# Where the output-weight conversions of block 0 stand in ScalarE's queue: behind the Silu of two chunks earlier

## The chip, the cores and the metric

The kernel runs on one core of a Trainium2 chip. The metric is the device time of one launch in microseconds (us). Before the change it is 964.89 us, the median of three runs (964.42 to 965.96).

## What is computed

An attention layer and two gated feed-forward layers follow each other, all in float32. Attention has 4 batches, 8 heads, 576 positions and a head size of 64; four heads look at the last 32 positions, four at every 32nd. Its output, 2304 tokens of 512 numbers, goes through two layers with a hidden size of 1536:

```python
x  = attention(q, k, v)                                        # (2304, 512)
xn = x / sqrt(mean(x * x, -1) + 1e-6) * rms_g
x  = (silu(xn @ w_gate) * (xn @ w_val)) @ w_out                # layer 1
out = ((x @ w_a) * (x @ w_b)) @ w_out2                         # layer 2
```

## The kernel before

**Blocks and chunks.** Layer 1 runs over six blocks of 384 tokens (`t`, line 742) and, inside a block, over twelve chunks of 128 hidden units (`fc`, line 755). For a chunk, TensorE makes `g_ps` and `v_ps`, 12 matmuls each (lines 759 and 761), VectorE scales `g_ps` into `sg` (line 774), ScalarE applies Silu to `sg` (line 776), VectorE multiplies it into `v_ps` (line 787), and `split` makes two parts of the result, `hl`: ScalarE casts the high part (line 506), VectorE in block 0 and GpSimd later subtract it for the low part (line 507). `emit_y` then multiplies `hl` with the chunk's output weights, 12 matmuls into four accumulators `y`. It is called one chunk late (line 783). `g_ps` and `v_ps` share three PSUM buffers, so a `v_ps` can begin only when an earlier buffer was read.

**Three matmuls for one.** Every float32 operand is a high and a low part; `mm3` (lines 481 to 483) multiplies high by high, high by low and low by high.

**The conversions.** The weights arrive in a 64-bit layout and are made into such parts once, in block 0. `conversion` (line 153) has five instructions: on ScalarE an in-place Prelu (line 137) and a copy of a half word into the scratch tile `cz` (line 142), on VectorE a shift and or (line 145), on ScalarE the cast of the high part (line 150), on GpSimd the subtraction for the low part (line 151). The gate and value weights of a chunk are converted together by `convert1`, 1024 words a row, one chunk ahead (line 764). The output weights, 512 words a row, are converted at the end of a chunk's program text (lines 790 to 792), through a single scratch tile, and stored to DRAM for the later blocks (line 793). Their raw words of chunks 0 to 7 lie in pairs in `gv_raw`; those of chunks 8 to 11 go through two buffers `raw`, so that the load of chunk 10 waits for the shift of chunk 8, and that of chunk 11 for the shift of chunk 9.

**Attention in between.** While block `t` runs, attention for block `t + 1` runs between its chunks (`attention_slot`, line 781): scores, exponentials on ScalarE (lines 264 and 336), transposes through one PSUM buffer `att` (line 358), copies of these out to `pt` (line 368). Exponential, Silu and square root need different tables in ScalarE, and a table load stands wherever the kind changes.

**What sets the order.** Nothing is written in queue order. The framework's scheduler arranges the instructions of each engine with a model of their times; every engine then runs its queue strictly in that order. The text can only add edges: `tc.issue_after(i)` makes the instructions of a `with` block that run on the engine of `i` stand behind `i` in its queue. `gate` uses it for steps of attention, and `behind` for the Silus, whose instructions are collected in the list `silu`:

```python
with gate(fc + 1), behind(silu[:1] if fc > 1 else []):
    run(conversion(raw.pop((fc, 2)), wt, pool, engine(WLO[fc][2]), LOW[fc][2], True))
```

`silu[:1]` is the Silu of chunk 0. In block 0 the Silu of a chunk is appended before its conversion is traced.

**Afterwards** come blocks 1 to 5 with reloaded output weights, and layer 2 with a Strassen-like scheme of seven products.

Of the kernel before, what the change touches and what calls it, by code (L numbers as in the profile page):

```python
# [77 lines left out]
def fused_kernel(ctx: ExitStack, tc: tile.TileContext, qtl, ktl, vl, qs, ks, vs, cst, w1, w2, out):  # L78
# [7 lines left out]
    def engine(c):  # L86
        return {"P": nc.gpsimd, "D": nc.vector}[c]
# [65 lines left out]
    def conversion(third, ready, pool, lo_eng, low, out=False):  # L153

        st = {}
        n = ready.shape[1] // 2

        def z():
            if not st:
                st["z"] = pool.tile([128, (1 if out else 2) * DM], U32, tag=f"cz{out}", name="cz", bufs=NCZ[out])  # L160
            return st["z"][:, :n * DM]

        def last():
            x = z().bitcast(F32).rearrange("p (a n) -> p a n", a=n)
            hl = ready.rearrange("p (a s) n -> p a s n", s=2)
            parts(x, hl[:, :, 0], hl[:, :, 1], lo_eng)

        return words(third, z, low=low) + [last]

    def run(steps):  # L170
        for f in steps:
            f()
# [312 lines left out]
    def mm_in(ps, w, sel, x):  # L485
        for cc in range(NCC):
            c = slice(cc * 128, (cc + 1) * 128)
            mm3(ps, w[:, sel, 0, c], w[:, sel, 1, c], x[cc][:, 0], x[cc][:, 1], cc == 0, cc == NCC - 1)

    def tmp(name):  # L490
        return act.tile([128, NTB], F32, tag="t", name=name, bufs=NTMP)

    made = []
    silu, silu_gate = [], []

    @contextmanager
    def behind(instructions):

        with ExitStack() as e:
            for i in instructions:  # L500
                e.enter_context(tc.issue_after(i))
            yield

    def split(h, lo_eng):
        hl = act.tile([128, 2, NTB], F32R, tag="hl", name="hl", bufs=3)
        made.append(nc.scalar.copy(hl[:, 0], h).ins)  # L506
        made.append(lo_eng.tensor_tensor(hl[:, 1], h, hl[:, 0].bitcast(F32), op=ALU.subtract).ins)  # L507
        return hl
# [26 lines left out]
    def load_units(n):  # L535
        for which in units[:n]:
            raw.update(zip(which, load_pair(w1, which)))
        del units[:n]

    def load_late(which):  # L540
        raw.update(zip(which, load_pair(w1, which, pool)))

    def convert1(fc):
        t = gv[fc] = gv_slot(F32R, "gv")
        two = [raw.pop((fc, k)) for k in range(2)]
        if fc in FUSEDW:
            both, ready = gvraw[fc], t.rearrange("p k a n -> p (k a) n")
            run(conversion(both.rearrange("p k a n -> p (k a) n"), ready, pool, engine(WLO[fc][0]), LOW[fc][0]))
        else:
            run(zipped(*(conversion(two[k], t[:, k], pool, engine(WLO[fc][k]), LOW[fc][k]) for k in range(2))))  # L550

    def wo_tile():
        return wop.tile([128, 2, DM], F32R, tag="wo", name="wo", bufs=3)
# [27 lines left out]
    @contextmanager  # L581
    def gate(fc):

        with behind(silu[:1] if fc > 4 else []), ExitStack() as e:
            for key in GATES[min(fc, len(GATES) - 1)].split():
                e.enter_context(tc.issue_after(s0["st"][key].ins))
            yield
# [7 lines left out]
    def emit_y(t, fc):  # L595
        if fc == 0:
            for e in range(NCC):
                y[t, e] = psum.tile([128, 512], F32, tag=f"y{e}", name=f"y{e}")
        h = hl.pop((t, fc))
        w = wo.pop((t, fc))  # L600
        for e in range(NCC):
            c = slice(e * 128, (e + 1) * 128)
            mm3(y[t, e][:, :NTB], w[:, 0, c], w[:, 1, c], h[:, 0], h[:, 1], fc == 0, fc == NFC - 1)

    def evac_y(t):
        for e in range(NCC):
            if e % 2 == 0:
                both = act.tile([128, 2, NTB], F32, tag="x", name="ys", bufs=8)
            ys = both[:, e % 2]
            nc.vector.tensor_tensor(ys, y[t, e][:, :NTB], ri[t], op=ALU.mult)  # L610
            nc.sync.dma_start(x2d[t, e // 2][:, e % 2], ys)

    def load_wo(t, fc):
        wt = wo[t, fc] = wo_tile()
        nc.sync.dma_start(wt.rearrange("p a n -> p (a n)").bitcast(F32), wod[fc])
# [5 lines left out]
    def attention_slot(steps, fc):  # L621
        st = steps["strided"]
        n_sl = 10
        if t == 0:
            part = strided1.get(fc, "").split()
        else:
            part = st[len(st) * fc // n_sl:len(st) * (fc + 1) // n_sl] if fc < n_sl else []
        part += local[min(t, 1)].get(fc, "").split()
        part += ["rms", "rinv"] * (fc == n_sl)
        for n in part:  # L630
            steps[n]()

    def exps(steps):

        def together(f, key):
            def g():
                with behind([silu[-1]]):
                    f()
                silu_gate.append(steps["st"][key].ins)
            return g  # L640

        for n in ("lexp0", "lexp1", "lexp2"):
            steps[n] = together(steps[n], "exp")
# [98 lines left out]
    for t in range(NB):  # L742
        if t == 1:
            apool.close()
            pool = apool.enter_context(tc.tile_pool(name="attn", bufs=1))
        if t == NB - 1:
            apool.close()
            cpool.close()
            pool = p2.enter_context(tc.tile_pool(name="forms", bufs=1, reuse_waits="tile"))
            early = [f for k in (4, 5, 0, 1, 2, 3) for f in convert_forms(k, k < 4)]  # L750
        nxt = attention(t + 1, pool, psum, itertools.cycle(["att"])) if t + 1 < NB else None
        if t == 0:
            exps(nxt)
        x = [xt[t, cc] for cc in range(NCC)]
        for fc in range(NFC):
            if t > 0 and fc == 0:
                load_wo(t, 0)
            g_ps = psum.tile([128, 512], F32, tag="gv", name="g_ps", bufs=3)
            mm_in(g_ps[:, :NTB], gv[fc], 0, x)
            v_ps = psum.tile([128, 512], F32, tag="gv", name="v_ps", bufs=3)  # L760
            mm_in(v_ps[:, :NTB], gv[fc], 1, x)
            if t == 0 and fc + 1 < NFC:
                with gate(fc + 1):
                    convert1(fc + 1)
                if fc + 2 == NFC:
                    load_late([(NFC - 2, 2), (NFC - 1, 2)])
            if t == NB - 1:
                slab[fc] = wgt.tile([128, 4 * DM], F32 if fc in (0, 1, 11) else F32R, tag="gv", name="slab", bufs=NFC)
                with behind(made):
                    run(early[len(early) * fc // NFC:len(early) * (fc + 1) // NFC])  # L770
                    for k in [k for k in x0 if k <= fc]:
                        run(x0.pop(k))
            sg = tmp("sg")
            nc.vector.tensor_tensor(sg, g_ps[:, :NTB], ri[t], op=ALU.mult)  # L774
            with behind(silu_gate):
                silu.append(nc.scalar.activation(sg, sg, AF.Silu).ins)  # L776
            silu_gate[:] = []
            if fc == 1 and t > 0:
                evac_y(t - 1)
            if nxt is not None:  # L780
                attention_slot(nxt, fc)
            if prev is not None:
                emit_y(*prev)
            if t > 0 and fc + 1 < NFC:
                load_wo(t, fc + 1)
            h = tmp("h") if t else v_ps[:, :NTB]
            made[:] = [nc.vector.tensor_tensor(h, sg, v_ps[:, :NTB], op=ALU.mult).ins]
            hl[t, fc] = split(h, engine(HLO0[fc] if t == 0 else HLO[t]))
            if t == 0:
                wt = wo[0, fc] = wo_tile()  # L790
                with gate(fc + 1), behind(silu[:1] if fc > 1 else []):
                    run(conversion(raw.pop((fc, 2)), wt, pool, engine(WLO[fc][2]), LOW[fc][2], True))
                nc.sync.dma_start(wod[fc], wt.rearrange("p a n -> p (a n)").bitcast(F32))
                if fc % 2 and units:
                    load_units(1)
            prev = (t, fc)
# [240 lines left out]
```

## Time and profile before

| | value |
|---|---|
| median of three runs | 964.89 us |
| profiled execution, whole | 967.4 us |
| its span from first to last instruction | 965.6 us |
| TensorE busy (matmul) | 937.1 us, 97% of the span |
| VectorE, ScalarE, GpSimd busy | 621.5, 425.3, 539.5 us |
| mean granted TensorE clock | 0.985 |
| the chain that ended last | TensorE 65%, DMA 11%, VectorE 7%, GpSimd 7%, ScalarE 4% |

Block 0's chunks run from about 34 to 133 us of the span. The share of busy time is a mean over the whole kernel; a change in block 0 is read in block 0, from the waits of TensorE there.

### The profile page before, as it was taken

Reading aid. Unit: us, or ns where it says so; the run is one execution under the profiler, and the core shown is the slowest. Engines: PE = TensorE matmul, PEld = TensorE weight load, DVE = VectorE, ACT = ScalarE, POOL = GpSimd, SP = SyncE. Lnnn points to the kernel's source line nnn. Section 1 sums busy time; section 2 is a strip of 40 time slices with the busy share of each in tenths; the row PEclk is TensorE's granted clock in tenths of the full one; section 3 lists DMA queues with packets and bytes.
Section 4 is the critical chain, followed back from the end, with each engine's and each line's share of the span. In section 5 each row is a group of like instructions: output and inputs, shape, how many; then the busy total and the mean of one; then the engine's idle time right before and its main releaser. Section 6 shows DMA issues by size and latency. Waiting matters only on the chain.

```text
span 965.6 us, 14099 instructions
## 1 busy us (share of the span) xinstructions
PE 937.1 (97%) x5318; PEld 888.2 (92%) x5318; DVE 621.5 (64%) x900; ACT 425.3 (44%) x795; POOL 539.5 (56%) x407
## 2 busy tenths in 40 slices
PE   5998999999999999999999899999999999999998
PEld 4898999999999999999999898899999998999996
DVE  5658858658819895986666378658655655564534
ACT  5988646344433434434555455436425422122110
POOL 3567946558649677878479545655724423123211
PEclk6899999999999999999999999999999999999999
DMA  9974286537535563532788884996993974754701
GB/s 342 408 262 151 89 288 218 151 96 225 165 104 161 161 204 102 185 105 87 284 324 306 329 306 166 402 415 247 385 373 114 345 274 165 284 205 168 267 2 66
DMA packets 57363, 215.55 MB, mean 223 GB/s; under 512 B 5968, under 2 KB 14544, under 8 KB 51664
## 3 DMA queue, kind: packets, MB, share of 16 engines
q1 hardware_dynamic: 57296, 214.66, 61.3%
q8 instruction: 42, 0.69, 0.3%
q14 instruction: 25, 0.20, 0.1%
HBM read 172.17 MB, written 42.47 MB: 222 GB/s over the span
## 4 chain that ended last, share of the span: by engine, by line
PE 65%; DMA 11%; DVE 7%; POOL 7%; ACT 4%; issue 4%; SPq 0%; DVEq 0%; ACTq 0%; POOLq 0%
PE o L916 5%; PE o L918 5%; PE o L917 5%; DMA raw<-in_w 4%; POOL prod L248 4%; PE Y L862 4%; PE Y L861 4%; PE Y L860 4%; DMA gv_raw<-in_w 3%; PE y L482 3%; PE y L481 3%; PE g_ps L483 3%; PE y L483 3%; PE g_ps L482 3%; PE g_ps L481 3%
## 5 line engine op out<-in xcount | busy, mean ns | idle before, releaser
L151 POOL TENSOR_TENSOR hl<-c,hl 128x384 fp32r<-128x384 f32 x72 | 77.9, 1082 | 181.0 <-ACT hl L150 174.4
L248 POOL TENSOR_TENSOR prod<-kv_t,qs_t 128x512 f32<-128x512 f32 (+12 forms) x57 | 108.3, 1921 | 15.3 <-DMA kv_t<-in_ks 8.2
L481 PE MATMUL v_ps<-xx,gv 128*128 128x384 f32 x288 | 97.7, 339 | 1.9 <-DVE sg L774 1.8
L482 PE MATMUL y<-hl,wo 128*128 128x384 f32 x288 | 98.1, 341 | 1.1 <-POOL hl L507 1.1
L281 POOL TENSOR_TENSOR prod<-kv_t,S_t 128x512 f32<-128x512 f32 (+12 forms) x57 | 86.2, 1526 | 21.1 <-issue 7.1
L482 PE MATMUL v_ps<-xx,gv 128*128 128x384 f32 x288 | 97.9, 340 | 0.0
L483 PE MATMUL v_ps<-xx,gv 128*128 128x384 f32 x288 | 97.8, 340 | 0.0
L481 PE MATMUL g_ps<-xx,gv 128*128 128x384 f32 x288 | 97.5, 339 | 0.0
L483 PE MATMUL g_ps<-xx,gv 128*128 128x384 f32 x288 | 97.3, 338 | 0.0
L482 PE MATMUL g_ps<-xx,gv 128*128 128x384 f32 x288 | 96.9, 337 | 0.0
L867 DVE TENSOR_TENSOR c<-c,Y 128x384 f32<-128x384 f32 x108 | 59.0, 551 | 58.8 <-PE Y L862 53.5
L507 POOL TENSOR_TENSOR hl<-h,hl 128x384 fp32r<-128x384 f32 x60 | 64.1, 1069 | 58.4 <-ACT hl L506 57.3
L483 PE MATMUL y<-hl,wo 128*128 128x384 f32 x288 | 95.0, 338 | 0.0
L284 DVE TENSOR_REDUCE xs_t<-prod 128x64 f32<-128x448 f32 (+17 forms) x57 | 85.7, 1521 | 9.7 <-POOL prod L281 9.5
L481 PE MATMUL y<-hl,wo 128*128 128x384 f32 x288 | 85.0, 343 | 7.0 <-ACT hl L506 5.4
L916 PE MATMUL o<-slab,hl 128*128 128x512 f32 x216 | 84.7, 393 | 1.8 <-DVE slab L925 1.3
L917 PE MATMUL o<-slab,hl 128*128 128x512 f32 x216 | 84.5, 392 | 0.0
L918 PE MATMUL o<-slab,hl 128*128 128x512 f32 x216 | 83.2, 394 | 0.0
L150 ACT CAST hl<-c 128x384 fp32r<-128x384 f32 x72 | 37.0, 514 | 93.8 <-DVE c L897 93.5
L776 ACT ACTIVATE sg<-sg 128x384 f32<-128x384 f32 x72 | 38.0, 528 | 86.4 <-DVE sg L774 86.0
L862 PE MATMUL Y<-slab,form 128*128 128x384 f32 x216 | 73.0, 338 | 0.0
L861 PE MATMUL Y<-slab,form 128*128 128x384 f32 x216 | 73.0, 338 | 0.0
(137 smaller groups left out, 2491.4 us busy)
## 6 DMA issues: line engine op xcount, KB each, us to landing
form<-formd SPq DMA_DIRECT2D x32, 1792.0 KB, 10.7
wo<-wod SPq DMA_DIRECT2D x60, 512.0 KB, 3.8
raw<-in_w SPq DMA_DIRECT2D x40, 512.0 KB, 7.3
gv_raw<-in_w SPq DMA_DIRECT2D x32, 512.0 KB, 10.2
formd<-form SPq DMA_DIRECT2D x6, 1792.0 KB, 7.5
formd<-forms SPq DMA_DIRECT2D x6, 1792.0 KB, 12.8
slab<-x2d SPq DMA_DIRECT2D x24, 384.0 KB, 4.0
wod<-wo SPq DMA_DIRECT2D x12, 512.0 KB, 3.4
```

Source lines behind the costliest of these rows:

```text
L151: lo_eng.tensor_tensor(lo, x, hi.bitcast(F32), op=ALU.subtract)
L248: nc.gpsimd.tensor_tensor(pr, st["ks", g][:, :, :n, :], st["qs"][:, heads(g), mm:mm + 1, :].to_broadcast([128, G, n, D]), op=ALU.mult)
L281: st["pvm"] = nc.gpsimd.tensor_tensor(pr, st["vs", g][:, :, :n, :], st["S"][:, heads(g), mm, :n, None].to_broadcast([128, G, n, D]), op=AL ...
L284: st["pvr"] = nc.vector.tensor_reduce(st["xs"][:, mm, heads(g), :], pr.rearrange("p g n d -> p g d n"), axis=X, op=ALU.add)
L481: nc.tensor.matmul(out_ps, w_hi, x_hi, start=start, stop=False)
L482: nc.tensor.matmul(out_ps, w_hi, x_lo, start=False, stop=False)
L483: nc.tensor.matmul(out_ps, w_lo, x_hi, start=False, stop=stop)
L861: nc.tensor.matmul(bank(n), hi, x[p][:, 1, c], start=False, stop=False, skip_group_check=not begins)
L862: nc.tensor.matmul(bank(n), lo, x[p][:, 0, c], start=False, stop=c == 1, skip_group_check=not begins)
L916: nc.tensor.matmul(o, h[:, 0, cols], w[0], start=n == 0, stop=False)
L917: nc.tensor.matmul(o, h[:, 0, cols], w[1], start=False, stop=False)
L918: nc.tensor.matmul(o, h[:, 1, cols], w[0], start=False, stop=n == len(chunks) - 1)
```

## The change

From chunk 3 on, the ScalarE instructions of the output-weight conversion of chunk n must stand behind the Silu of chunk n - 2. For chunk 2 nothing changes: both rules name the Silu of chunk 0. Nothing is computed differently, and no instruction is added or taken away, except that the scheduler, given the new edges, arranges all queues anew up to the middle of block 1.

```diff
-                with gate(fc + 1), behind(silu[:1] if fc > 1 else []):
+                with gate(fc + 1), behind(silu[max(fc - 2, 0):max(fc - 1, 1)] if fc > 1 else []):
                     run(conversion(raw.pop((fc, 2)), wt, pool, engine(WLO[fc][2]), LOW[fc][2], True))
```

In the queues below, `sg_451`, `sg_529`, `sg_614`, `sg_847` and `sg_938` belong to chunks 0, 1, 2, 5 and 6; `hl_485` and `hl_891` to chunks 0 and 5; `v_ps_431` and `v_ps_509` to chunks 0 and 1. `gv_raw_179`, `gv_raw_188` and `gv_raw_197` hold the raw output weights of chunks 2 and 3, 4 and 5, 6 and 7, and `raw_203` those of chunk 8. The other `gv_raw`, 1024 wide, are gate and value weights.

ScalarE, from the Silu of chunk 0 to the cast of its result, before:

```order
L776 ACTIVATE sg_451<-sg_451 128x384
L137 ACTIVATE gv_raw_179<-gv_raw_179 128x512
L142 ACTIVATE cz_657<-gv_raw_179 128x512
L137 ACTIVATE gv_raw_179<-gv_raw_179 128x512
L137 ACTIVATE gv_raw_191<-gv_raw_191 128x1024
L137 ACTIVATE gv_raw_188<-gv_raw_188 128x512 x2
L776 ACTIVATE sg_529<-sg_529 128x384
L150 CAST gv_689<-cz_691 128x2x512
L137 ACTIVATE gv_raw_194<-gv_raw_194 128x1024
L506 CAST hl_485<-v_ps_431 128x384
```

and now:

```order
L776 ACTIVATE sg_451<-sg_451 128x384
L137 ACTIVATE gv_raw_179<-gv_raw_179 128x512
L142 ACTIVATE cz_657<-gv_raw_179 128x512
L137 ACTIVATE gv_raw_191<-gv_raw_191 128x1024
L776 ACTIVATE sg_529<-sg_529 128x384
L137 ACTIVATE gv_raw_179<-gv_raw_179 128x512
L150 CAST gv_689<-cz_691 128x2x512
L137 ACTIVATE gv_raw_194<-gv_raw_194 128x1024
L506 CAST hl_485<-v_ps_431 128x384
```

Two Prelus of 512 words (chunks 4 and 5) have left this stretch, and a third (chunk 3) moved behind the Silu of chunk 1.

VectorE at the same place, before:

```order
L787 TENSOR_TENSOR v_ps_431<-sg_451,v_ps_431 128x384
L145 SCALAR_TENSOR_TENSOR cz_657<-gv_raw_179,cz_657 128x512
L774 TENSOR_TENSOR sg_614<-g_ps_581,rinv_403 128x384
L787 TENSOR_TENSOR v_ps_509<-sg_529,v_ps_509 128x384
L507 TENSOR_TENSOR hl_485<-v_ps_431,hl_485 128x384
```

and now:

```order
L787 TENSOR_TENSOR v_ps_431<-sg_451,v_ps_431 128x384
L145 SCALAR_TENSOR_TENSOR cz_657<-gv_raw_179,cz_657 128x512
L787 TENSOR_TENSOR v_ps_509<-sg_529,v_ps_509 128x384
L774 TENSOR_TENSOR sg_614<-g_ps_581,rinv_403 128x384
L507 TENSOR_TENSOR hl_485<-v_ps_431,hl_485 128x384
```

The scaling of chunk 2 (line 774) now stands behind the product of chunk 1 (line 787), which waits for the Silu of chunk 1.

ScalarE, from the Silu of chunk 5 to the cast of its result, before:

```order
L776 ACTIVATE sg_847<-sg_847 128x384
L368 COPY pt0_114<-att_866 96x8x64
L142 ACTIVATE cz_1115<-gv_raw_725 128x1024
L137 ACTIVATE gv_raw_902<-gv_raw_902 128x1024
L776 ACTIVATE sg_938<-sg_938 128x384
L506 CAST hl_891<-v_ps_827 128x384
```

and now:

```order
L776 ACTIVATE sg_847<-sg_847 128x384
L137 ACTIVATE gv_raw_197<-gv_raw_197 128x512
L137 ACTIVATE gv_raw_902<-gv_raw_902 128x1024
L264 ACT_TABLE_LOAD
L264 ACTIVATE S_t_456<-S_t_456 128x72
L368 COPY pt0_114<-att_866 96x8x64
L142 ACTIVATE cz_1115<-gv_raw_725 128x1024
L776 ACT_TABLE_LOAD
L776 ACTIVATE sg_938<-sg_938 128x384
L137 ACTIVATE raw_203<-raw_203 128x512
L142 ACTIVATE cz_982<-gv_raw_197 128x512
L506 CAST hl_891<-v_ps_827 128x384
```

Two table loads, the exponential of the strided scores (line 264) and three instructions of the conversions of chunks 6, 7 and 8 now stand between the Silu of chunk 5 and the cast of its result; before, the exponential and its two table loads stood behind the casts of chunks 5 and 6. On TensorE the first four matmuls of chunk 5's `emit_y` stood ahead of `v_ps` of chunk 7 and stand behind it now.

## Rows read from the trace of the kernel before

**Rows 1.** Waits of TensorE, 33 to 140 us: us in total, times, longest.

```profile
PE y L481 <- ACT hl L506: 5.4, 3, 2.1
PE v_ps L481 <- DVE sg L774: 1.8, 3, 1.0
PE att L358 <- ACT pt L368: 0.7, 1, 0.7
```

**Rows 2.** Windows of TensorE: stretch, length, busy, granted clock, DMA share, GB/s.

```profile
53.00:57.00 4.00, 4.00 (x16) 0.57 1.05 401
90.50:94.50 4.00, 3.84 (x14) 0.57 0.73 262
131.00:135.00 4.00, 2.62 (x15) 1.00 0.73 235
```

**Rows 3.** Timeline of TensorE, 47 to 52 us: start, duration, instruction, idle before, releaser.

```profile
47.57 0.44 PE L481 MATMUL v_ps<-xx,gv 128*128 128x384 f32 x1 [0.65 <-DVE sg L774]
51.78 0.97 PE L481 MATMUL y<-hl,wo 128*128 128x384 f32 x4 [1.85 <-ACT hl L506]
```

**Rows 4.** Timeline of ScalarE, 45 to 52 us.

```profile
45.65 0.66 ACT L142 ACTIVATE cz<-gv_raw 128x512 uint32<-128x512 uint16 x1
46.20 2.80 ACT L137 ACTIVATE gv_raw<-gv_raw 128x512 f32<-128x512 f32 x4
48.87 0.55 ACT L776 ACTIVATE sg<-sg 128x384 f32<-128x384 f32 x1
...
51.23 0.50 ACT L506 CAST hl<-v_ps 128x384 fp32r<-128x384 f32 x1
```

**Rows 5.** Timeline of VectorE, 46 to 50 us.

```profile
46.96 0.56 DVE L774 TENSOR_TENSOR sg<-g_ps,rinv 128x384 f32<-128x384 f32 x1
49.45 0.56 DVE L787 TENSOR_TENSOR v_ps<-sg,v_ps 128x384 f32<-128x384 f32 x1 [1.93 <-ACT sg L776]
```

**Rows 6.** Waits of ScalarE, 33 to 140 us.

```profile
ACT s_t L336 <- DVE lmx L323: 2.7, 2, 1.7
```

**Rows 7.** Timeline of ScalarE, 84 to 95 us.

```profile
84.58 1.28 ACT L776 ACT_TABLE_LOAD   x1
85.87 0.53 ACT L776 ACTIVATE sg<-sg 128x384 f32<-128x384 f32 x1
...
87.82 1.12 ACT L137 ACTIVATE gv_raw<-gv_raw 128x1024 f32<-128x1024 f32 x1
88.83 0.51 ACT L776 ACTIVATE sg<-sg 128x384 f32<-128x384 f32 x1
89.25 0.45 ACT L506 CAST hl<-v_ps 128x384 fp32r<-128x384 f32 x1
...
93.86 0.27 ACT L264 ACTIVATE S_t<-S_t 128x72 f32<-128x72 f32 x1
```

**Rows 8.** Timeline of TensorE, 87 to 91 us.

```profile
87.01 0.61 PE L358 MATMUL att<-cst_sb,s_t 128*96 128x128 f32 x4 [0.71 <-ACT pt L368]
89.75 0.96 PE L481 MATMUL y<-hl,wo 128*128 128x384 f32 x4 [2.13 <-ACT hl L506]
90.88 0.69 PE L481 MATMUL v_ps<-xx,gv 128*128 128x384 f32 x1 [0.16 <-DVE sg L774]
```

**Rows 9.** Timeline of VectorE: end of the normalization, conversions of chunks 8 and 9.

```profile
96.33 0.23 DVE L273 TENSOR_TENSOR S_t<-S_t,srs 128x72 f32<-128x72 f32 x1
...
106.77 2.92 DVE L145 SCALAR_TENSOR_TENSOR cz<-raw,cz 128x512 uint32<-128x512 uint32 x1
...
118.68 1.32 DVE L145 SCALAR_TENSOR_TENSOR cz<-raw,cz 128x512 uint32<-128x512 uint32 x1
```

**Rows 10.** The end of block 0: timelines of ScalarE, the DMA queue and TensorE.

```profile
117.52 0.68 ACT L142 ACTIVATE cz<-raw 128x512 uint32<-128x512 uint16 x1 [1.70 <-POOL wo L151]
...
120.03 0.33 SPq L111 DMA_DIRECT2D raw<-in_w  x1
...
132.83 0.96 PE L481 MATMUL y<-hl,wo 128*128 128x384 f32 x4 [1.39 <-ACT hl L506]
```

## Prediction

> **What bounds the kernel now.** I read the page first: TensorE is busy 97% of the span, so only its idle time and its low-clock time can be won or lost. Then the waits of TensorE in block 0 [rows 1]: 5.4 us for the casts of `hl`, 1.8 us for the scaling that frees a PSUM buffer, 0.7 us for a copy of the transposes. The windows [rows 2] show what else is lost: in 53 to 57 us and in 90.5 to 94.5 us the granted clock was 0.57, a stretch at the lower level, 1.2 GHz, in each; everywhere else in the chunks it was at or near 2.4 GHz. One such stretch costs 43% of 4 us, about 1.7 us of work. Before the first TensorE had stood still 1.85 us in one piece [rows 3], before the second 2.13 us and 0.71 us [rows 8]; the idle 1.39 us at the end of the block [rows 10] was followed by a clock of 1.00 [rows 2]. So all that block 0 can give is some 8 us of waits and 3 us of clock. From 135 to 240 us the list of TensorE's waits is empty, and the queues differ only up to the middle of block 1 (some 190 us), so a lead or lag at 133 us should go through to the end.
>
> The sum is made against the profiled execution, 967.4 us with a span of 965.6; the median of the runs, 964.89, is 2.5 below it, and I carry the difference over. About 0.2%, 1.9 us, is what a measurement of this kernel can tell from no change.
>
> **The first place, chunks 0 to 2.** ScalarE's stretch from the Silu of chunk 0 to the cast of its result loses two Prelus of 512 words. One such piece takes 0.55 us from start to start (45.65 to 46.20) [rows 4]. So the cast moves from 51.23 to 50.1 us, 1.1 us earlier, and the Silu of chunk 1 (three Prelus fewer ahead of it) from 48.87 to 47.2. That alone would take 1.1 us from the wait of 1.85 us. But VectorE now does the product of chunk 1 first, and that waits for this Silu: 47.2 and 0.55 for the Silu [rows 4] is 47.75, the product 0.5 to the next start, then the scaling of chunk 2, 0.56 [rows 5], ends at 48.8 where it ended at 47.5 before. `v_ps` of chunk 2 waits for exactly this scaling and so starts 1.3 us later than 47.57 [rows 3]. TensorE's idle time is therefore 0.65 + 1.30 = 1.95 us in one piece ahead of `v_ps`, and none ahead of `y`, whose `hl` has been ready since 50.6: 1.95 against 0.65 + 1.85 = 2.50 us. **Gain 0.55 us**, bounds 0 (the Silu no earlier) and 1.1 (the product does not hold the scaling). A still stand of 1.95 us lies between the two that came before a fall (1.85, 2.13) and above the one that did not (1.39), so I let the clock fall as before, at no gain.
>
> **The second place, chunks 5 to 7.** Ahead of the Silu of chunk 5, ScalarE has three Prelus fewer in its queue than before (chunks 7, 8 and 9), 1.7 us; its waits for the scores, 2.7 us in all [rows 6], take part of that back, since those come from TensorE and VectorE. Between 0 and 1.7 I take 0.9: the Silu at 85.0 instead of 85.87 [rows 7]. Behind it the queue got longer. The cast of chunk 5's `hl` came 3.38 us after the Silu (85.87 to 89.25). Now two table loads of 1.28, an exponential of 0.27 and three conversion pieces of 0.55 come on top: 3.38 + 2.56 + 0.27 + 1.65 = 7.9 us, so 92.9 us.
>
> More of this lies on TensorE's path. The copy to `pt`, which frees the buffer of the transposes, comes after the exponential: 85.0 + 0.42 (Silu) + 0.55 + 1.01 (the wide Prelu, 87.82 to 88.83) + 1.28 + 0.2 = 88.5, done at 89.0 us. TensorE would be done with chunk 7's `g_ps` at 86.30 - 0.55 = 85.75 and waits 3.4 us instead of 0.71 [rows 8]. After 0.61 us of transposes `v_ps` of chunk 7 waits for its scaling, which stands on VectorE behind the normalization of the strided scores. That ran from 94.13 (end of the exponential) to 96.56 [rows 7, 9] with a product of 0.5 in it; without that some 1.8 us: 88.7 + 1.8 + 0.56 is 91.0, against 90.88 before. So the lead is gone there, and the first four matmuls of chunk 5's `y`, 0.96 us, which ran inside the wait before, come after. **Lag behind before: about 1 us**, that is 1.5 us lost here. Bounds: nothing lost if the Silu leads by 1.7 us, 2.4 lost if by none. The clock falls here before and after: once each, at no cost.
>
> The Trainium skill has a rule against just this: its page ScalarE: Activation LUTs, section "Table sets: the hidden batching unit", says to do all functions of one set before switching, and section "What ACT_TABLE_LOAD costs" gives 1283 ns for the load and about 1380 ns for a drain. The trace agrees with the load (1.28 us) and not with the drain: the Silu starts 0.01 us after the load ends [rows 7]. By the Trainium skill's 2.66 us for each switch the pair would put another 2.8 us, an estimate, on the path.
>
> **The end of the block.** Before, TensorE stood 1.39 us for the cast of chunk 11 [rows 10]. That wait takes up a lag of up to 1.39 us as long as the cast does not come later. Its chain begins with the shift of chunk 9 (118.68, [rows 9]), which frees the buffer for the load of chunk 11 (120.03), and runs over the conversions of chunks 10 and 11, the square root and two table loads, one after the other, to 132.83. The shift itself waited for chunk 8's subtraction on GpSimd, 1.70 us [rows 10]. In the new queue of GpSimd two score products stand ahead of the conversions instead of between them, so this wait can shrink; but all else arrives 1 us later. I take the cast as 0.4 us earlier; bounds 1.7 earlier (no wait), 1.6 later (the shift takes 2.92 instead of 1.32 us, as chunk 8's did [rows 9]). TensorE is free at 131.4 + 1.0 = 132.4, and the cast is there at 132.4. **Sum: +0.55 - 1.5 + 1.39 of cover, so 0.4 us gained**, 964.89 - 0.4 = 964.5 us. The other edits (queues of block 1, two reloads of output weights issued later) I cost at nothing: TensorE has no wait there, and it would show as a new one.
>
> **Rivals.** *The clock holds at the first place.* The still stand comes in one piece ahead of `v_ps`, with full work around it. If it does not bring the lower clock, 1.7 us are won on top of 0.55. ScalarE's chain lets not all of it through; with 1.8 us of 2.25 the time is 963.1. Against it: both falls of before followed a pause of about this size. Chance 0.27.
>
> *ScalarE becomes the bound between the Silus of chunks 5 and 6* and the kernel is slower. If the Silu of chunk 5 does not lead, `v_ps` of chunk 7 starts at 91.9, the lag is 1.9 us, and TensorE has stood still some 5 us in two pieces instead of 3.0, so that a second low-clock stretch of 1.7 us follows. 3.6 us less 1.39 of cover is 2.2 more: 967.1 us. It decides from the point where the lag passes 1.39 us, a Silu of chunk 5 later than about 85.4. For it: the scores set ScalarE's pace [rows 6]. Chance 0.15.
>
> *The shift of chunk 9 is held up by GpSimd*, as chunk 8's was (2.92 us). The cast then comes 1.2 us late instead of 0.4 early: 966.1 us. Against it: chunk 9's took 1.32 before. Chance 0.10. The Trainium skill (page SBUF — State Buffer, section "SBUF: two separate sides") has VectorE operations with two SBUF inputs and GpSimd share one port pair that the first holds for its whole instruction; the trace has both durations, and does not show the port.
>
> *A table switch costs more than its row*, a pause as long as the load after each: 2 x 1.28 more, at 1.0 + 2.56 - 1.39 a lag of 2.2: 967.1. Nothing in the trace speaks for it; chance 0.02. The drain that the Trainium skill states (ScalarE: Activation LUTs, "What ACT_TABLE_LOAD costs") would be such a pause.
>
> **How the numbers follow.** The forecast, 964.5, has 0.46, with its own range from 963.5 to 965.8. The first rival straddles the bound of 1.9 us: 0.18 of its 0.27 I count as faster, and 0.08 of the forecast through its bounds. So faster 0.26; slower takes the second rival, the fourth and a part of the others, 0.21; same 0.53. Leaving out 2 in 10 the range is 962.4 to 967.2.
>
> **What would show it.** Right: the wait ahead of `v_ps` of chunk 2 about 1.95 us and none ahead of the first `y`; the cast of chunk 5 about 7.9 us after its Silu; a wait of some 3.4 us for the copy to `pt`; the last wait of block 0 short or gone; the end of the block within 1 us of 132.8. Wrong: a clock near 1.00 in 50 to 57 us, or a third low stretch, or new waits in block 1 for reloaded weights.

## The result, and the profile after

The changed kernel takes 974.34 us (median of four runs, 972.54 to 975.19), the kernel before on the same chip 965.42 us (964.42 to 966.67). The ratio is 1.0086, 95% interval 1.0071 to 1.0101: **slower by about 8.3 us** (8.9 by the medians), where 964.5 was forecast and 967.2 was the upper end of the range. The profiled execution took 972.54 us with a span of 970.8, mean granted clock 0.987.

The waits of TensorE from 33 to 200 us, in the profile of the changed kernel (us in total, times, longest):

```profile
PE att L358 <- ACT pt L368: 3.8, 1, 3.8
PE v_ps L481 <- DVE sg L774: 3.2, 3, 1.7
PE att L296 <- DVE s_t L314: 1.5, 1, 1.5
PE y L481 <- ACT wo L150: 1.5, 1, 1.5
PE g_ps L481 <- DVE sg L774: 1.3, 1, 1.3
PE att L358 <- DVE s_t L348: 1.0, 1, 1.0
PE y L482 <- POOL hl L507: 1.0, 2, 0.5
PE y L481 <- DVE ys L610: 0.4, 1, 0.4
PE att L412 <- ACT sq L432: 0.2, 1, 0.2
```

Against [rows 1]: the 5.4 us for the casts of `hl` are gone, 3.8 us for the copy to `pt` have come, and seven kinds of wait are new. Four of these, 3.9 us, lie in block 1, where the list of before was empty; none of them is for reloaded output weights (`wo` at 113 us is chunk 8's conversion in block 0). The first two windows of [rows 2]:

```profile
53.00:57.00 4.00, 4.00 (x25) 1.00 1.05 403
90.50:94.50 4.00, 4.00 (x19) 0.70 0.54 179
```

The clock held at the first place and fell at the second. The timeline of TensorE at its longer waits:

```profile
48.13 0.45 PE L481 MATMUL v_ps<-xx,gv 128*128 128x384 f32 x1 [1.73 <-DVE sg L774]
...
82.39 0.41 PE L481 MATMUL g_ps<-xx,gv 128*128 128x384 f32 x1 [1.28 <-DVE sg L774]
...
88.53 0.61 PE L358 MATMUL att<-cst_sb,s_t 128*96 128x128 f32 x4 [3.79 <-ACT pt L368]
...
89.44 0.67 PE L481 MATMUL v_ps<-xx,gv 128*128 128x384 f32 x1 [0.29 <-DVE sg L774]
...
113.45 0.44 PE L481 MATMUL y<-hl,wo 128*128 128x384 f32 x1 [1.46 <-ACT wo L150]
...
156.18 1.15 PE L296 MATMUL att<-k_t,q_t 128*64 128x64 f32 x16 [1.49 <-DVE s_t L314]
...
172.33 0.61 PE L358 MATMUL att<-cst_sb,s_t 128*96 128x128 f32 x4 [1.01 <-DVE s_t L348]
```

ScalarE at the second place, to set beside [rows 7]:

```profile
84.26 0.53 ACT L776 ACTIVATE sg<-sg 128x384 f32<-128x384 f32 x1
...
86.36 1.28 ACT L264 ACT_TABLE_LOAD   x1
...
87.83 0.56 ACT L368 COPY pt<-att 96x512 f32<-96x512 f32 x1
...
89.45 1.28 ACT L776 ACT_TABLE_LOAD   x1
90.74 0.53 ACT L776 ACTIVATE sg<-sg 128x384 f32<-128x384 f32 x1
...
92.33 0.45 ACT L506 CAST hl<-v_ps 128x384 fp32r<-128x384 f32 x1
```

**Where the lag arises.** Two milestones place it. The first is the start of `v_ps` of block 1's second chunk, with all of block 0 behind it: 137.12 us before and 137.60 now, a lag of 0.5. The second is a scaling in the middle of block 1, after which the two queues agree to the end; the timeline of VectorE has it before, and then in the changed kernel, as

```profile
200.59 0.56 DVE L774 TENSOR_TENSOR sg<-g_ps,rinv 128x384 f32<-128x384 f32 x1 [1.78 <-PE g_ps L483]
```

```profile
206.27 0.56 DVE L774 TENSOR_TENSOR sg<-g_ps,rinv 128x384 f32<-128x384 f32 x1 [1.78 <-PE g_ps L483]
```

a lag of 5.7. So of the pair of profiled executions block 1 costs 5.2 us, and block 0 next to nothing. That pair flatters block 0: the execution of before had lost some 1.6 us to the clock at the first place, which the changed one had not.

The listed waits of block 1 sum to 3.9 us; most of the rest of the 5.2 lies at the same stops, which cost more than the list counts. The 12 matmuls of one `y` took 2.08 us up to the next `g_ps` before (175.02 to 177.10 us) and take 2.88 now (179.90 to 182.78), with a listed wait of 0.51.

How block 1 loses this shows on VectorE. In the changed kernel's timeline, the fourth evacuation of block 0's output stands behind a reduction of strided scores, and two normalizations behind reductions of strided products:

```profile
135.36 1.48 DVE L610 TENSOR_TENSOR ys<-y,rinv 128x384 f32<-128x384 f32 x3
140.01 0.62 DVE L251 TENSOR_REDUCE S_t<-prod 128x7 f32<-128x448 f32 x1 [3.17 <-POOL prod L248]
140.55 0.55 DVE L610 TENSOR_TENSOR ys<-y,rinv 128x384 f32<-128x384 f32 x1
...
170.64 1.00 DVE L284 TENSOR_REDUCE xs_t<-prod 128x64 f32<-128x512 f32 x1
171.56 2.03 DVE L348 TENSOR_TENSOR s_t<-s_t,lrs 128x384 f32<-128x384 f32 x2
```

Before, all four evacuations ran ahead of that reduction, and the normalizations ahead of the first reduction of strided products, which began at 165.81 us:

```profile
136.41 1.94 DVE L610 TENSOR_TENSOR ys<-y,rinv 128x384 f32<-128x384 f32 x4
...
163.67 1.15 DVE L348 TENSOR_TENSOR s_t<-s_t,lrs 128x384 f32<-128x384 f32 x1
```

GpSimd's first product of the block waits for a load of keys. The queue of DMA issues (SP) now has a reload of output weights between two of the three key loads; the first row is of before, the others of the changed kernel:

```profile
132.86 1.70 SPq L236 DMA_DIRECT2D kv_t<-in_ks  x3
...
133.39 1.19 SPq L236 DMA_DIRECT2D kv_t<-in_ks  x2
134.68 0.37 SPq L615 DMA_DIRECT2D wo<-wod  x1
135.09 0.43 SPq L236 DMA_DIRECT2D kv_t<-in_ks  x1
```

The product starts at 138.82 us (137.75 before), 1.1 later. The first key load was issued 0.5 later anyway, so about half of this goes with the reload; no run tried it alone.

### The profile page after: what moved, and what is told of

It is laid out like the page before. It is cut to its first block, busy times and chain, and to the rows that moved or that the text cites. A ratio compares the mean times of both kernels' runs of the same rounds, so it can differ in the third digit from the quotient of the medians.

```text
span 970.8 us, 14102 instructions
## 1 busy us (share of the span) xinstructions
PE 936.3 (96%) x5318; PEld 886.0 (91%) x5318; DVE 622.7 (64%) x900; ACT 424.4 (44%) x795; POOL 542.6 (56%) x407
## 4 chain that ended last, share of the span: by engine, by line
PE 65%; DMA 9%; POOL 8%; DVE 8%; ACT 4%; issue 4%; SPq 0%; POOLq 0%; DVEq 0%; ACTq 0%
PE o L916 5%; PE o L918 5%; PE o L917 5%; POOL prod L248 4%; DMA raw<-in_w 4%; PE Y L862 4%; PE Y L861 4%; PE Y L860 4%; PE y L482 3%; DMA gv_raw<-in_w 3%; PE y L481 3%; PE y L483 3%; PE g_ps L483 3%; PE v_ps L481 3%; PE v_ps L483 3%
## 5 line engine op out<-in xcount | busy, mean ns | idle before, releaser
L248 POOL TENSOR_TENSOR prod<-kv_t,qs_t 128x512 f32<-128x512 f32 (+12 forms) x57 | 106.3, 1888 | 25.6 <-DMA kv_t<-in_ks 18.2
```

The source lines that it names most:

```text
L248: nc.gpsimd.tensor_tensor(pr, st["ks", g][:, :, :n, :], st["qs"][:, heads(g), mm:mm + 1, :].to_broadcast([128, G, n, D]), op=ALU.mult)
```

## The experiments

All kernels but e6, e9 and e10 differ from the kernel before only in the Silu behind which the conversion of a chunk queues; a table in the line of the change says it, and a chunk that the table does not name stays behind the Silu of chunk 0:

```diff
-  behind(silu[:1] if fc > 1 else [])
+  behind(silu[{3: 1, 4: 1, 5: 1}.get(fc, 0):][:1] if fc > 1 else [])
```

Theory A puts more than half of the loss into block 1's new order; theory B puts it into block 0, between the Silus of chunks 5 and 6. Which order block 1 takes follows from the scheduler, and some tables leave it as before while others change it; that made the parts separable.

| run | table or edit | median us | ratio to before, 95% interval | lag at the two milestones, us |
|---|---|---|---|---|
| the change | n - 2 | 974.34 | 1.0086 (1.0071 to 1.0101) | 0.5, 5.7 |
| e1 | 3, 4, 5: 1 | 965.79 | 0.9997 (0.9989 to 1.0006) | -2.3, -2.3 |
| e2 | as e1, 7: 5 | 967.11 | 1.0015 (1.0006 to 1.0023) | -0.1, -0.1 |
| e3 | 8: 6, 9: 7 | 971.41 | 1.0055 (1.0043 to 1.0067) | 2.6, 5.5 |
| e4 | 7: 5 | 966.98 | 1.0012 (1.0003 to 1.0020) | -0.7, -0.7 |
| e5 | 3: 1, 4: 2, 5: 3, 8: 6, 9: 7 | 968.90 | 1.0030 (1.0020 to 1.0040) | 1.8, 1.9 |
| e6 | the change, one edge more in block 1 | 973.75 | 1.0074 (1.0057 to 1.0091) | 3.0, 8.0 |
| e7 | 3: 1, 4: 2, 5: 2 | 968.74 | 1.0029 (1.0019 to 1.0040) | 2.0, 2.0 |
| e8 | 3, 4, 5: 1, 6: 3 | 967.53 | 1.0012 (1.0001 to 1.0024) | 0.2, 0.2 |
| e9 | the change, block 1: local steps first | 971.68 | 1.0062 (1.0045 to 1.0079) | 1.3, 3.7 |
| e10 | before, block 1: local steps first | 965.91 | 1.0002 (0.9986 to 1.0018) | -2.3, -2.3 |
| e11 | 3, 4, 5: 1, 11: 11 | 963.35 | 0.9974 (0.9960 to 0.9988) | order differs, -3.9 |
| e12 | 11: 11 | 963.13 | 0.9982 (0.9968 to 0.9996) | order differs, -3.3 |

A lag is of one profiled execution against that of before. Executions of the same queue differ by up to 1 us at the start of block 0, and by some 1.6 us more where the clock held at the first place, so the difference of a row's two lags says more than either.

**e1, the first place alone.**

> Chunks 3, 4 and 5 behind the Silu of chunk 1, all later ones behind that of chunk 0 as before: the queues differ from before on ScalarE and VectorE between the Silu of chunk 0 and that of chunk 2, and nowhere else. Theory A (the loss of the change was made in block 1's new queues) and theory B (it was made between the Silus of chunks 5 and 6) both expect the gain of the first place alone: if the clock holds there as in the profile of the changed kernel, 2.5 us less than before (962.9); if it falls in most runs, as in the prediction, 0.5 less (964.9). Theory C (the first place itself is worth nothing or costs over many runs): 965.4 or more.

No gain over the runs. The wait ahead of `v_ps` of chunk 2 was 1.72 us, as in the change, but 0.55 us for `hl` of chunk 0 stayed, since another order of ScalarE's pieces than in the change stands ahead of that cast. The profiled execution held its clock; e10, with the queue of before, held it as well. That is theory C's number, and the gain of 2.5 us is ruled out; a gain of 0.5 us lies inside the interval. The place is worth nothing that can be measured.

**e2 and e4, the exponential moved ahead with and without the first place.** The table of e4:

```diff
-  behind(silu[:1] if fc > 1 else [])
+  behind(silu[{7: 5}.get(fc, 0):][:1] if fc > 1 else [])
```

> As e1, and chunk 7 behind the Silu of chunk 5: the exponential of the strided scores now stands between the Silus of chunks 5 and 6, as in the change, and block 1 keeps the order of before. Theory A: the loss of the middle of block 0 is small, within 1 us of e1. Theory B: the loss between the Silus costs the 3.8 us that the profile of the change shows from 56 to 134 us: 3 to 4 us more than e1.

> Chunk 7 behind the Silu of chunk 5, the others as before: the first place and block 1 are those of before, the exponential stands between the Silus of chunks 5 and 6. Theory A: within 1 us of before (964.5 to 966.5). Theory B: 3 to 4 us slower (968.5 to 969.5).

Both lose 1.2 to 1.4 us, and nothing in block 1. Theory A's size is right within half a microsecond; B's 3 to 4 us do not come. In these two the copy to `pt` stands ahead of the exponential, and TensorE waits only 1.26 and 1.23 us for it. It also waits 1.54 us for a scaling ahead of a `g_ps` and 2.01 for the one ahead of `v_ps` of chunk 7: 4.8 us at this place in both, against 3.0 in the kernel before [rows 8] and 5.4 in the change.

**e3, the late chunks alone.** Table `{8: 6, 9: 7}`.

> Chunks 8 and 9 behind the Silus of chunks 6 and 7, the others as before: the first place is that of before, the exponential stands between the Silus of chunks 5 and 6, and block 1 has the new order of the change. Theory A: 4 to 5 us slower than before by block 1's waits alone, 969.5 to 970.5 and up. Theory B: as slow, but with the lag already there at the end of block 0. The lag at 134 us tells them apart: under 1.5 us for A, 3 or more for B.

The time is as both expected, and neither has the place: 2.6 us at the end of block 0 and 2.9 more in block 1. Both theories have a half of it. Its order of block 1 is not quite that of the change, as the expectation had it: VectorE's two normalizations stand behind three reductions of strided products instead of five, and the wait of 1.01 us at 172 us is absent.

**e5, block 1 given back its order.** Chunks 6, 7, 10 and 11 return to the Silu of chunk 0:

```diff
-  behind(silu[max(fc - 2, 0):max(fc - 1, 1)] if fc > 1 else [])
+  behind(silu[{3: 1, 4: 2, 5: 3, 8: 6, 9: 7}.get(fc, 0):][:1] if fc > 1 else [])
```

> The change for chunks 3, 4, 5, 8 and 9; chunks 6, 7, 10 and 11 stay behind the Silu of chunk 0. The first place is that of the change, the exponential stands between the Silus of chunks 5 and 6 and ahead of the copy to pt as in the change, but block 1 has the order of before. Theory A (more than half of the loss is block 1's new order): within 2 us of e2, 966 to 969. Theory B (the loss is made in block 0 behind the Silu of chunk 5): close to the change, 972 to 975.

2.9 us slower than before instead of 8.3: more than half of the loss went with block 1's order. (Block 0 is not exactly that of the change either: the wait of 1.46 us for chunk 8 is absent, and the one ahead of `v_ps` of chunk 7 is longer.) All waits of its TensorE from 33 to 200 us:

```profile
PE v_ps L481 <- DVE sg L774: 4.8, 3, 1.9
PE att L358 <- ACT pt L368: 3.9, 1, 3.9
PE y L481 <- ACT hl L506: 0.8, 1, 0.8
PE g_ps L481 <- DVE sg L774: 0.6, 1, 0.6
```

Nothing is left in block 1, and the 3.9 us at the copy to `pt` stand as in the change. Against e1, which differs only in block 0, e5 with the exponential ahead of the copy costs 3 us, and e2 with the copy ahead 1.3. That the place of the copy makes this difference is not shown: e5 also moves chunks 8 and 9, and its profile lost the clock at the first place, which that of e1 held.

**e6, one wait of block 1 taken away.** In `attention_slot`:

```diff
-            steps[n]()
+            with behind([silu[{'lexp0': 14}[n]]] if t == 1 and n in {'lexp0': 14} else []): steps[n]()
```

> The change with one edge more, in block 1: the first exponentials of the local scores stand behind the Silu of block 1's chunk 2 again, as before, so that this Silu does not wait for two table loads; VectorE's product behind it and the scaling of the second group of scores behind that follow. Theory A: the wait of 1.49 us for that scaling at 156 us shrinks or goes, 0.5 to 1.5 us less than the change (973 to 974). Theory B: no difference over 0.5 us. If the wait was set by the score products on GpSimd instead: no difference either, and the wait stays.

The wait at 156 us fell to 0.77, but the one at 172 us rose from 1.01 to 1.49. Two thirds of the gain were given back there, and the times don't part this run from the change.

**e7 and e8, other places for the exponential.** Tables `{3: 1, 4: 2, 5: 2}` and `{3: 1, 4: 1, 5: 1, 6: 3}`.

> Chunk 3 behind the Silu of chunk 1, chunks 4 and 5 behind that of chunk 2; the others as before. The first place is that of the change, ScalarE takes the Silu of chunk 6 and the cast of chunk 5 ahead of the exponential, and block 1 is that of before. If a shorter stretch from the Silu of chunk 5 to its cast shortens TensorE's waits at 85 to 95 us: 1 to 2 us less than before (964 to 965). If the pair of table loads behind the cast of chunk 5 only moves the wait to the cast of chunk 6: as before, 965 to 966.5.

> Chunks 3, 4 and 5 behind the Silu of chunk 1, chunk 6 behind that of chunk 3, the others as before. The first place is as in e1, the exponential and its table loads stand between the cast of chunk 5 and the Silu of chunk 7, block 1 is that of before. By the reading that the table loads hurt where they stand between a Silu and its cast: not slower than e1 (964 to 966). If any move of the exponential to the front costs: 967, as e2.

Both are slower than before, so neither of the first alternatives came, nor e7's second; e8's second, 967, did. In e7 the copy to `pt` came late again (a wait of 3.82 us), though the cast of chunk 5 was early and the copy stood ahead of the pair of table loads. It stood behind two casts, a wide Prelu, the Silu of chunk 6 and a wide copy to `cz`:

```profile
88.06 0.56 ACT L368 COPY pt<-att 96x512 f32<-96x512 f32 x1
...
89.01 1.28 ACT L264 ACT_TABLE_LOAD   x1
```

In e7 the clock also fell at the end of block 0: 0.66 from 135 to 139 us, behind a wait of 1.79 us for the cast of chunk 11. In e8 the wait for the copy was 0.62 us, but 2.23 us for a scaling (`g_ps`) came ahead of it.

**e9 and e10, the order inside block 1's slots.** The same edit on the change and on the kernel before:

```diff
-        part += local[min(t, 1)].get(fc, "").split()
+        part = local[1].get(fc, "").split() + part if t == 1 else part + local[min(t, 1)].get(fc, "").split()
```

> The change, and in block 1 the steps of local attention stand ahead of the strided ones in each slot of the text. Block 0's queues are those of the change to the last row; in block 1 VectorE's normalizations of the local scores come ahead of the strided reductions that wait for GpSimd. Theory A (more than half of the loss is block 1's new order): the waits at 156 and 172 us shrink or go, 1.5 to 3 us less than the change, 971 to 973; the lag against before at 134 us stays that of the change, and less is added behind it. Theory B (block 0): no change, 974.

> The kernel before with the same edit of block 1's slots and nothing else. If the edit only mends what the change broke, it is worth nothing here, since the normalizations stand ahead already: 965.4 to 966.4. If it is worth something by itself, 1 us or more either way, and e9 is to be read against that.

On the change it gives 2.7 us by the medians (2.3 by the ratios, whose intervals overlap at their ends, so that the times alone don't settle it), on the kernel before nothing. The profile shows the mechanism. TensorE's waits from 134 to 200 us in e9:

```profile
PE att L296 <- DVE s_t L314: 0.7, 1, 0.7
PE y L481 <- DVE ys L610: 0.5, 1, 0.5
PE y L482 <- POOL hl L507: 0.5, 1, 0.5
PE y L481 <- ACT hl L506: 0.2, 1, 0.2
```

and VectorE's normalizations, ahead of the strided reductions again:

```profile
166.43 1.14 DVE L348 TENSOR_TENSOR s_t<-s_t,lrs 128x384 f32<-128x384 f32 x2
...
170.04 2.09 DVE L284 TENSOR_REDUCE xs_t<-prod 128x64 f32<-128x448 f32 x2 [1.10 <-POOL prod L281]
```

Block 0's queues are those of the change in this run, and the lag added in block 1 falls from 5.2 to 2.4 us.

**e11 and e12, chunk 11 behind its own Silu.** The table of e12, to which e11 adds that of e1:

```diff
-  behind(silu[:1] if fc > 1 else [])
+  behind(silu[{11: 11}.get(fc, 0):][:1] if fc > 1 else [])
```

> Chunks 3, 4 and 5 behind the Silu of chunk 1, and chunk 11 behind the Silu of chunk 11; the others as before. Block 0 up to chunk 10 is that of e1. The Silu of chunk 11 no longer waits for the last conversion, so TensorE's wait of 1.4 us at the end of block 0 goes, and block 1 gets an order of its own. If new orders of block 1 are costly by their nature: 968 or more. If it depends on the order: 964 to 965.5.

> Chunk 11 behind the Silu of chunk 11, all others as before: the queues of e11 but for the first place, which is that of before. If e11's gain is the wait at the end of block 0 (1.4 us) with what its order of block 1 brings: as fast as e11 against before, ratio 0.997 to 0.999. If the first place carries it: 1.000.

Both beat the kernel before, by 0.3% and 0.2%, and so the change; they can't be told apart, and as e1 was worth nothing the gain is that of chunk 11. The waits of e11 from 33 to 200 us are all of them in block 0:

```profile
PE v_ps L481 <- DVE sg L774: 3.0, 3, 1.8
PE y L481 <- ACT hl L506: 2.1, 1, 2.1
PE att L358 <- ACT pt L368: 0.4, 1, 0.4
```

The 1.39 us at the end of block 0 [rows 10] are gone, for the last conversion now stands behind the Silu. ScalarE in e12:

```profile
125.67 0.53 ACT L776 ACTIVATE sg<-sg 128x384 f32<-128x384 f32 x1
...
127.43 0.48 ACT L506 CAST hl<-v_ps 128x384 fp32r<-128x384 f32 x1
128.06 0.62 ACT L150 CAST wo<-cz 128x512 fp32r<-128x512 f32 x1
```

Block 1 has an order of its own here too, and loses nothing by it: a new order is not costly as such.

## Why the prediction was wrong

**The step that failed** is "The other edits (queues of block 1, two reloads of output weights issued later) I cost at nothing: TensorE has no wait there, and it would show as a new one." It did show: block 1 lost 5.2 us in the pair of profiles, 5.4 as the ratio of the change less that of e5, more than half of the loss. In the six runs that leave block 1 its order (e1, e2, e4, e5, e7, e8) the lag grows by 0.1 us at most there. The prediction's own sign, "new waits in block 1 for reloaded weights", had the place and not the cause: TensorE's new waits are for VectorE's and GpSimd's attention work and evacuations. That a stretch has no waits says that its old order fits, not that a new one will. The differences could have been read beforehand in the two kernels' queues: on VectorE normalizations and an evacuation behind reductions that wait for GpSimd, on SP the reload between the key loads.

**The first place** came as worked out in the profile, but for the clock. The wait ahead of `v_ps` of chunk 2 was 1.73 us (1.95 forecast), none stood ahead of the first `y`, the cast came at 49.45 us (50.1). The clock held, which was the first rival. Its price was right (1.7 us forecast; from the first `y` to the scaling of chunk 3 it took 6.1 us before, 51.78 to 57.86, and 4.5 in e10, 50.94 to 55.41, 1.6 apart), but to make it a consequence of the change was wrong: e4, e10 and e12 held it with the queue of before, e5, e6, e7 and e11 lost it with the new one.

**The second place.** The cast of chunk 5 came 8.07 us after its Silu (7.9 forecast), the Silu at 84.26 (85.0), the wait for the copy to `pt` was 3.79 us (3.4), and `v_ps` of chunk 7 started at 89.44 (91.0), so the chain on ScalarE was right; on VectorE the normalization of the strided scores took 0.9 us (87.95 to 88.83) and not 1.8. The term "lag behind before: about 1 us", 1.5 us lost, was too small. The waits from 81 to 91 us sum to 5.4 us against 3.0 before [rows 8], 2.4 lost: the 1.28 us at 82 us for the scaling of an earlier chunk had no step in the sum. It stands on VectorE behind the strided scores, which the new order takes earlier.

**The end of the block.** The wait for chunk 11 went and gave its 1.39 us back, as forecast. Ahead of it, 1.46 us for the converted weights of chunk 8 at 113 us came with no step for them: only the shift of chunk 9 was looked at, and chunk 8's conversion, which moved too, became the late one (its shift began at 109.87 us, 106.77 before [rows 9]). In e5, where block 1 costs nothing and chunk 8 is in time, block 0 still lost 2.9 us: 3.9 us at the copy to `pt`, 1.9 more ahead of `v_ps` of chunk 7. So the sum for block 0, 0.4 gained, was off by some 3 us too; with block 1's 5.2 this is about the whole 8.3.

**The rivals.** The slower rival, ScalarE between the Silus of chunks 5 and 6 at 967.1 us, has the right sign and, by e4 (1.2 us) and e5 against e1 (3 us), about the right size for block 0. Its condition, a Silu of chunk 5 later than 85.4 us, was not met in the change (84.26), and no second low-clock stretch followed there, so that its size is right in part by luck. In e5 the Silu came at 86.83 us, TensorE stood 6.3 us there, and the low clock lasted longer (0.50 from 90 to 94 us, 0.70 from 94 to 98). The rival on the shift of chunk 9 did not come: that shift took 1.03 us, and chunk 8's 2.87 as before (2.92), only later. A table switch that costs more than its row is not borne out: the Silu at 90.74 us starts 0.01 us after the load of 1.28 ends. The Trainium skill (ScalarE: Activation LUTs, section "Table sets: the hidden batching unit") says to finish one set's functions before switching. No run here tests that rule, for before and after have three loads each from 82 to 102 us. What the change altered is when the pair runs, and with it when the copy runs that TensorE waits for; whether the copy stands ahead of the pair does not decide the wait alone (1.26 us in e2 and 3.82 in e7, both with the copy ahead; 3.79 in the change with it behind).

What stays open: how the 2.4 us that e9 leaves in block 1 divide between the late key load and the order on GpSimd, since no run moved the load alone; and how block 0's 3 us divide between the second place and chunk 8.

## What to carry to other kernels

Where a scheduler arranges the queues, a small new edge is a new schedule for everything behind it: read the whole difference of every queue, as far as it goes, and give each instruction that moved behind one that waits for another engine a price, also where the old profile shows no wait. Then try several edges with the same local effect, and choose by what they do to the rest; here they lay between 0.997 and 1.009. An edge that clears one wait and leaves the next block's order harmless (chunk 11 behind its own Silu) was worth more than the rule for all chunks.

## What was not expected of the hardware

The granted clock at the first place is not a property of the queue. Windows of TensorE, 53 to 57 us, of e10 and then of e3, whose queues there are both those of before:

```profile
53.00:57.00 4.00, 4.00 (x25) 1.00 1.05 400
```

```profile
53.00:57.00 4.00, 4.00 (x16) 0.57 1.05 402
```

Of the fourteen profiles, six fell to the lower level there and eight held the upper one (2.4 GHz); with the new queue (e5, e6, e7 and e11) the fall came earlier, between 48 and 54 us. Ahead of it the longest still stand had been 1.79 to 1.96 us in those that fell and 1.62 to 1.75 in those that held; with the queue of before it was 1.85 and 1.82 (fell: before, e3) and 1.62, 1.63 and 1.66 (held: e4, e10, e12). Whether the length of the stand is cause or sign was not tried; executions of one queue differ by as much.

The times of the kernel before point the same way. Of its 96 runs that stand beside the experiments, 46 have a mean granted clock of 0.988 or more and a median time of 965.1 us, and 45 have 0.986 or less and a median of 966.8 us. The two groups are 1.7 us apart, the price of one low stretch; that it was the first place in each of them no trace shows. A gain or loss of that size at one such place is not to be forecast from a single profile.
